# Four-token sums of q and k of the first sequence: by TensorE from the loaded rows, in place of VectorE from the transposed ones

## The chip, the cores and the metric

The kernel runs on one core of a Trainium2 chip. The metric is the time of one execution on the device in microseconds (us), the median of three runs. TensorE (PE), VectorE (DVE), ScalarE (ACT), GpSimd (POOL) and SyncE (SP) each work through a queue of their own, in order; SP only issues DMAs here.

## What is computed

Attention over 2 sequences of 576 tokens with 8 heads of width 64, then two mixtures of experts over the 1152 tokens. Cut to what matters:

```python
q_d = q.reshape(B, H, Sd, factor, D).mean(axis=3)      # factor = 4, Sd = 144
k_d = k.reshape(B, H, Sd, factor, D).mean(axis=3)
v_d = v.reshape(B, H, Sd, factor, D).mean(axis=3)
out_up = np.repeat(sm_attn(q_d, k_d, v_d), factor, axis=2)
mask = np.abs(pos[:, None] - pos[None, :]) < factor     # a narrow band
out_local = np.matmul(softmax(where(mask, scale * q @ k.T, -1e9)), v)
x = _moe_ref(out_up + out_local, **moe)                 # 4 experts, all of them for every token
return _moe2_ref(x, **moe2)                             # 8 experts, one for each token
```

## The kernel before

The attention works on pairs of heads. Pair n (0 to 3 are the first sequence, 4 to 7 the second) is loaded as `kraw` and `qraw`: each in two halves of tokens, f = 0 and 1, on 98 partitions with 3 tokens x 2 heads x 64 values each. `tr` transposes a half on TensorE in three matmuls against the identity into a bank of PSUM, `t_copy` brings the bank to SBUF as `kT` or `qT` (channels on partitions, 292 tokens), on ScalarE or VectorE.

From there two branches start. The coarse branch needs sums over four neighbouring tokens: `pool4` makes them from kT and qT, as one reduction on VectorE (L434) or two additions on GpSimd, 72 sums for each half. `down` then makes the scores of the sums (`d1_mm`, L466), their softmax (minimum on VectorE, exponentials on ScalarE, the product `da` on VectorE, L487), transposes it (`d2_tr`, L492), multiplies with the sums of v (`d3_mm`, L504) and copies to `od`. The local branch (`scores`, L544; `l2_tr`, L579; `l3_mm`, L595) makes the band's softmax in units (pair, half): (0), (1) and then (2, 3) together for half 0, (0, 1) and (2, 3) for half 1. `l3_add` joins both branches to `xf`, and `x_hi`, `x_lo` split that into `xhi`, `xlo`, the two parts in which the first mixture (L693: `mm1`, L712 to L714: `mm2`) takes its input. Slice kk of `xhi` holds pair kk; a product over all of a chunk's 512 features needs all four pairs.

The first mixture needs the weights as `w1h`, `w1l`, `w2h`, `w2l`: a copy on ScalarE (L414) and a difference on VectorE (L673), or other engines.

What sets the order is the planner `Plan`: each operation has an engine or several to choose from, a cost, what it reads and writes and a priority; `order` lists the operations as they would start by those costs, and the program issues them in that order, each engine's queue in order. While the plan's clock is under 100 us it also puts **fillers** in front of an operation of TensorE that it sees waiting: matmuls of a constant (L1590) whose result nobody reads, to keep TensorE's clock up. A buffer named in `new` is waited for by the planner; PSUM has 7 banks for it. The second sequence's attention is planned among the first mixture's products. After the plan the rest of the first mixture is a plain loop, and the second mixture has plans of its own.

Of the kernel before, what the change touches and what calls it, by code (L numbers as in the profile page):

```python
# [8 lines left out]
F32 = mybir.dt.float32  # L9
# [4 lines left out]
ALU = mybir.AluOpType  # L14
# [3 lines left out]
D = 64  # L18
HALF = S // 2
SD = S // 4  # L20
# [50 lines left out]
RP = 98  # L71
RR = 3
QOFF = S - RR * RP
# [14 lines left out]
TARGET = 3600  # L88
HARD = 3400
TRC = 1  # L90
RUNS = 0
TRR = .75
DP = (50, 20, 0)
DQ = (0, 0, 0, 0, 0, 0)
DMC = 1.23
# [195 lines left out]
def moe_chain_kernel(ctx, tc, q, k, v, probs, w1, w2, mod, wg, mbias, v1, v2, out):  # L291
    nc = tc.nc
# [12 lines left out]
    at = ctxa.enter_context(tc.tile_pool(name="at", bufs=2, side="right"))  # L305
# [7 lines left out]
    ident = const.tile([128, 128], F32, tag="ident", name="ident")  # L313
# [7 lines left out]
    def make_mask():  # L321
# [9 lines left out]
        nc.gpsimd.tensor_copy(out=mask16[0:64], in_=mask[0:64])  # L331
        nc.gpsimd.tensor_copy(out=mask16[64:128], in_=m1[64:128])

    def consts():
        P.op("Pool", .6, lambda: make_identity(nc, ident), w=["ident"], prio=-9)
        P.op("Pool", 1.2, make_mask, r=["ident"], w=["mask"], prio=-8)
        P.op("SP", .65, lambda: nc.sync.dma_start(out=p_raw, in_=probs.rearrange("(i p) e -> p i e", p=128)),
             w=["praw"], prio=8, lat=.5)
        P.op("DVE", .8, norm_p, r=["praw"], w=["p"], prio=30)
# [17 lines left out]
    T = {}  # L357
    LAST = {}

    def ch(nm, d):  # L360
        return {e: c for e, c in d.items() if (nm, e) not in NOT}


    def qk_dma(nm, src, n, f):
        b, hp = divmod(n, 4)
        if f == 0:
            T[nm, n] = at.tile([RP, 2, 2 * RR * D], F32, tag=nm + "raw", name=nm + "raw", bufs=RAWB)
        x = src[b, 2 * hp:2 * hp + 2, QOFF * f:QOFF * f + RR * RP]
        if n < RUNS:
            nc.sync.dma_start(out=T[nm, n][:, f].rearrange("p (h x) -> p h x", h=2), in_=x.rearrange("h (p r) d -> p h (r d)", r=RR))  # L370
        else:
            nc.sync.dma_start(out=T[nm, n][:, f].rearrange("p (r h d) -> p r h d", r=RR, h=2), in_=x.rearrange("h (p r) d -> p r h d", r=RR))

    def vq_dma(n):
        b, hp = divmod(n, 4)
# [12 lines left out]
    def a_load(n, pr):  # L388
        for f in range(2):
            for nm, src in (("k", k), ("q", q)):  # L390
                cost, lat = (.5, .5) if n < RUNS else (.84, .9)
                P.op("SP", cost, lambda nm=nm, src=src, f=f: qk_dma(nm, src, n, f), prio=pr, lat=lat, w=[(nm, n, f)],
                     **({"r": [(nm, n)]} if f else {"new": [(nm + "raw", (nm, n))]}))
        P.op("SP", .65, lambda: vq_dma(n), prio=pr, lat=.82, new=[("vq", ("vq", n))])

# [5 lines left out]
    def tr(nm, n, f):  # L401
        T["pt", nm, n, f] = pt = bank()
        pv = pt[:, 0:RR * RP].rearrange("c (p r) -> c r p", r=RR)
        for r in range(RR):
            x = T[nm, n][:, f]
            if n < RUNS:
                nc.tensor.transpose(pv[0:64, r, :], x[:, D * r:D * r + D], ident[:RP, :RP])
                nc.tensor.matmul(pv[64:128, r, :], x[:, D * (RR + r):D * (RR + r) + D], ident[:RP, :RP], start=True, stop=True)
            else:
                nc.tensor.transpose(pv[:, r, :], x[:, 128 * r:128 * r + 128], ident[:RP, :RP])  # L410

    def copy(e, out, in_, scale=1.0):
        if e is nc.scalar:
            e.activation(out=out, in_=in_, func=ACTF.Copy, scale=scale)  # L414
        elif scale == 1.0:
            e.tensor_copy(out=out, in_=in_)
        else:
            e.tensor_scalar(out=out, in0=in_, scalar1=scale, scalar2=None, op0=ALU.mult)

    def t_copy(e, nm, n, f):  # L420
        o = win(f, 0) - QOFF * f
        t = T[nm + "T", n, f] = at.tile([128, KW], F32, tag=f"{nm}T{f}", name=f"{nm}T{f}", bufs=(KT0, 4)[f])
        copy(e, t, T["pt", nm, n, f][:, o:o + KW], 1.0 if nm == "k" else -0.125)

    def pool4(e, nm, n, f):
        if f == 0:
# [21 lines left out]
    def a_tr(n, pr):  # L448
        for f in range(2):
            for nm in ("k", "q"):  # L450
                pt, xt = ("pt", nm, n, f), (nm + "T", n, f)
                P.op("PE", .27 if n >= RUNS else TRR, lambda nm=nm, f=f: tr(nm, n, f), cols=TRC * RR * RP * RP / 128, r=[(nm, n), (nm, n, f), "ident"],
                     new=[("ps", pt)] + ([(f"{nm}T{f}", xt)] if n > 3 else []), prio=pr)
                P.op(ch("kt", {"ACT": .3, "DVE": .38}), 0, lambda e, nm=nm, f=f: t_copy(e, nm, n, f), r=[pt], prio=pr,
                     **({"w": [xt]} if n > 3 else {"new": [(f"{nm}T{f}", xt)]}))
                P.op(ch("p4", {"DVE": .36, "Pool": .75}), 0, lambda e, nm=nm, f=f: pool4(e, nm, n, f), r=[xt], prio=pr,
                     **({"new": [(nm + "s", (nm + "s", n))]} if f == 0 else {"w": [(nm + "s", n)]}))
        P.op("Pool", VDC, lambda: a_vd(n), r=[("vq", n)], new=[("vd", ("vd", n))], prio=pr)
# [1090 lines left out]
    if True:  # L1549
        consts()  # L1550
        a_load(0, 0)
        for b in range(2):
            P.slow, P.lag, P.also = ((1.0, 0.0, {}), (SLOWB, LAGB, {"ps": ("pa",)}))[b]
            pa, pb = ((0, BP), (BQ, BR))[b]
            for us in GRP[2 * b]:
                for m in us:
                    n = 4 * b + m
# [43 lines left out]
        for s, c, f in steps[KP:]:  # L1601
# [3 lines left out]
            r = runs.index((s, c))  # L1605
# [61 lines left out]
```

## Time and profile before

| | us |
|---|---|
| median of three runs (lowest, highest) | 627.0 (625.95, 627.65) |
| the profiled execution | 624.6 |
| its span in the profile | 622.7 |
| PE busy in the span | 600.4 (96%) |
| DVE, ACT, POOL busy | 381.8, 255.2, 86.9 |
| first product of the first mixture starts | 42.37 |

The span is the profiled execution without some 2 us around it. A row of the timeline is one instruction or several of a kind in sequence: its start, how long it ran, engine, line, operation, what it writes and reads, how many records, and in brackets how long its engine sat idle just before and who ended that. Starts of neighbours on TensorE are closer than their durations, because matmuls overlap; what an instruction costs its engine is the distance to the next start. One fp32 matmul leaves two records, a transpose one.

### The profile page before, as it was taken

Reading aid. Unit: us, or ns where it says so; the run is one execution under the profiler, and the core shown is the slowest. Engines: PE = TensorE matmul, PEld = TensorE weight load, DVE = VectorE, ACT = ScalarE, POOL = GpSimd, SP = SyncE. Lnnn points to the kernel's source line nnn. Section 1 sums busy time; section 2 is a strip of 40 time slices with the busy share of each in tenths; the row PEclk is TensorE's granted clock in tenths of the full one; section 3 lists DMA queues with packets and bytes.
Section 4 is the critical chain, followed back from the end, with each engine's and each line's share of the span. In section 5 each row is a group of like instructions: output and inputs, shape, how many; then the busy total and the mean of one; then the engine's idle time right before and its main releaser. Section 6 shows DMA issues by size and latency. Waiting matters only on the chain. (4 is left out here: it accounts for less than half of the span.)

```text
span 622.7 us, 11280 instructions
## 1 busy us (share of the span) xinstructions
PE 600.4 (96%) x4265; PEld 527.5 (85%) x4270; DVE 381.8 (61%) x817; ACT 255.2 (41%) x595; POOL 86.9 (14%) x120
## 2 busy tenths in 40 slices
PE   7689999999999999999999999999999999999994
PEld 4578888889798999999989989999988898888983
DVE  4898678767525618564342455439955789669781
ACT  5855256542313411113321334313343555559581
POOL 3333113115000001000000000001130035201011
PEclk9999999999999999999999999999999999999997
DMA  7999944107511510001330345605295404867830
GB/s 148 156 219 221 234 135 136 36 2 213 168 35 61 177 34 2 1 1 52 119 101 1 102 135 173 200 5 132 42 352 193 143 15 131 286 194 254 293 136 20
DMA packets 84465, 78.67 MB, mean 126 GB/s; under 512 B 36135, under 2 KB 67248, under 8 KB 84402
## 3 DMA queue, kind: packets, MB, share of 16 engines
q1 hardware_dynamic: 82482, 73.13, 42.0%
q0 software_dynamic: 1920, 4.73, 2.2%
q8 instruction: 35, 0.57, 0.4%
q14 instruction: 28, 0.23, 0.1%
HBM read 77.49 MB, written 5.07 MB: 133 GB/s over the span
## 5 line engine op out<-in xcount | busy, mean ns | idle before, releaser
L693 PE MATMUL ps<-xhi,w1h 128*128 128x256 f32 (+1 forms) x512 | 153.8, 300 | 0.0
L693 PE MATMUL ps<-xhi,w1l 128*128 128x256 f32 (+1 forms) x512 | 151.8, 297 | 0.0
L693 PE MATMUL ps<-xlo,w1h 128*128 128x256 f32 (+1 forms) x512 | 151.6, 296 | 0.2 <-DVE xlo L609 0.2
L699 ACT ACTIVATE hh<-ps 128x256 fp32r<-128x256 f32 (+1 forms) x128 | 52.4, 410 | 209.6 <-PE ps L693 201.2
L704 DVE SCALAR_TENSOR_TENSOR hl<-ps,hh 128x256 fp32r<-128x256 f32 (+1 forms) x128 | 57.9, 454 | 121.2 <-ACT hh L699 121.0
L712 PE MATMUL ps<-w2h,hh 128*128 128x512 f32 x288 | 115.7, 402 | 0.0
L714 PE MATMUL ps<-w2h,hl 128*128 128x512 f32 x288 | 113.6, 395 | 1.2 <-DVE hl L704 1.2
L713 PE MATMUL ps<-w2l,hh 128*128 128x512 f32 x288 | 113.3, 393 | 0.0
L693 PEld LDWEIGHTS ps<-xhi,w1h 128*128 128x128 f32 x512 | 96.5, 188 | 5.9 <-issue 0.6
L693 PEld LDWEIGHTS ps<-xlo,w1h 128*128 128x128 f32 x512 | 96.4, 188 | 5.3 <-DVE xlo L609 0.4
L693 PEld LDWEIGHTS ps<-xhi,w1l 128*128 128x128 f32 x512 | 96.4, 188 | 0.0
L714 PEld LDWEIGHTS ps<-w2h,hl 128*128 128x128 f32 x288 | 54.0, 188 | 14.8 <-DVE hl L704 2.3
L712 PEld LDWEIGHTS ps<-w2h,hh 128*128 128x128 f32 x288 | 54.2, 188 | 8.0 <-issue 0.4
L713 PEld LDWEIGHTS ps<-w2l,hh 128*128 128x128 f32 x288 | 54.2, 188 | 6.9
L673 DVE TENSOR_TENSOR w2l<-raw,w2h 128x1024 fp32r<-128x1024 f32 x32 | 39.4, 1230 | 29.3 <-ACT w2h L414 29.2
L414 ACT ACTIVATE w1h<-raw 128x1024 fp32r<-128x1024 f32 x47 | 49.7, 1057 | 17.6 <-PE ps L693 14.9
L673 DVE TENSOR_TENSOR w1l<-raw,w1h 128x1024 fp32r<-128x1024 f32 x32 | 39.1, 1221 | 10.8 <-ACT w1h L414 10.1
L414 ACT ACTIVATE w2h<-raw 128x1024 fp32r<-128x1024 f32 x28 | 29.7, 1061 | 37.6 <-PE ps L714 35.6
L1222 DVE TENSOR_TENSOR w2l<-r,w2h 128x1024 fp32r<-128x1024 f32 x28 | 33.9, 1221 | 14.5 <-ACT w2h L414 14.5
L985 POOL DMA_INDIRECT tab<-tg,si x9 | 9.6, 1062 | 209.8 <-DVE tg L982 188.3
L414 ACT ACTIVATE w2h<-r 128x1024 fp32r<-128x1024 f32 x28 | 29.4, 1058 | 17.0 <-PE ps L1345 9.2
L1321 PE MATMUL ps<-xh,w1h 128*128 128x256 f32 x128 | 36.0, 281 | 0.0
(287 smaller groups left out, 933.1 us busy)
## 6 DMA issues: line engine op xcount, KB each, us to landing
raw<-in_moe_w_dram SPq DMA_DIRECT2D x85, 512.0 KB
r<-in_moe_w_dram SPq DMA_DIRECT2D x35, 512.0 KB
v<-in_v_dram SPq DMA_DIRECT2D x32, 80.0 KB
kraw<-in_k_dram SPq DMA_DIRECT2D x16, 147.0 KB
qraw<-in_q_dram SPq DMA_DIRECT2D x16, 147.0 KB
vq<-in_v_dram SPq DMA_DIRECT2D x8, 288.0 KB
ys<-y SPq DMA_DIRECT2D x9, 256.0 KB
st<-in_moe_w_gate_dram SPq DMA_DIRECT2D x4, 512.0 KB
```

The lines of the kernel that those rows point to most:

```text
L414: e.activation(out=out, in_=in_, func=ACTF.Copy, scale=scale)
L673: e.tensor_tensor(out=l, in0=W.pop(("raw", kind, s, j)), in1=h.bitcast(F32), op=ALU.subtract)
L693: nc.tensor.matmul(o, wt[:, kk, fs], xt[:, kk, :], start=(kk == 0 and m == 0), stop=(kk == KD - 1 and m == 2))
L699: nc.scalar.activation(out=hh, in_=o, func=ACTF.Relu)
L704: nc.vector.scalar_tensor_tensor(out=hl, in0=o, scalar=0.0, in1=hh.bitcast(F32), op0=ALU.max, op1=ALU.subtract)
L712: nc.tensor.matmul(a, hh[:, ts], hi[:, f % 2, :], start=(f == 0), stop=False)
L713: nc.tensor.matmul(a, hh[:, ts], lo[:, f % 2, :], start=False, stop=False)
L714: nc.tensor.matmul(a, hl[:, ts], hi[:, f % 2, :], start=False, stop=(f == NF - 1))
L985: i = nc.gpsimd.indirect_dma_start(out=tab, out_offset=bass.IndirectOffsetOnAxis(ap=Z["si"][:, t:t + 1], axis=0), in_=G["tg"][:, 3 * c + t ...
L1222: e.tensor_tensor(out=l, in0=R["raw", u], in1=h.bitcast(F32), op=ALU.subtract)
L1321: nc.tensor.matmul(pt, wt[:, kk, fs], xt[:, kk, :], start=(i == 0), stop=(i == 3 * KD - 1))
```

## The change

For the first sequence (n < 4) the sums come straight from the loaded rows. `make_pool` has GpSimd write a matrix of ones and zeros, `poolm`, that adds the right tokens; `tr` adds to the bank of half 1 six matmuls of `kraw` or `qraw` with it (three tokens of each partition for either half; together the 144 sums, at columns 300 to 443 of the bank); `pool_copy` brings the sums to `ks` or `qs` on ScalarE or VectorE; the `pool4` of these pairs goes. A memset of `qs` is GpSimd's now. The cost that the planner is told for such a `tr` rises by .75. Two options that were switched off (`RUNS`, `TRR`) go too.

```diff
-RUNS = 0
-TRR = .75
+PPN = 4
+PPC = .75
+POFF = 300
...
+    def make_pool():
+        for g in range(2):
+            off = QOFF * g - HALF * g
+            m = pool_m[:, g]
+            nc.gpsimd.memset(m, 1.0)
+            nc.gpsimd.affine_select(out=m, in_=m, pattern=[[1, RR], [-4, 72]], compare_op=ALU.is_ge, fill=0.0, base=off, channel_multiplier=RR)
+            nc.gpsimd.affine_select(out=m, in_=m, pattern=[[-1, RR], [4, 72]], compare_op=ALU.is_ge, fill=0.0, base=3 - off, channel_multiplier=-RR)
...
+        P.op("Pool", 1.6, make_pool, w=["pool"], prio=-7)
...
+        if f and n < PPN:
+            for g in range(2):
+                for r in range(RR):
+                    nc.tensor.matmul(pt[:, POFF + 72 * g:POFF + 72 * g + 72], T[nm, n][:, g, 128 * r:128 * r + 128], pool_m[:, g, r, :],
+                                     start=(r == 0), stop=(r == RR - 1))
...
+    def pool_copy(e, nm, n):
+        t = T[nm + "s", n] = at.tile([128, SD + 16], F32, tag=nm + "s", name=nm + "s")
+        if nm == "q":
+            nc.gpsimd.memset(t[:, SD:SD + 16], 0.0)
+        copy(e, t[:, 0:SD], T["pt", nm, n, 1][:, POFF:POFF + SD], 1.0 if nm == "k" else -0.125)
...
+                if n < PPN:
+                    if f:
+                        P.op({"ACT": .19, "DVE": .24}, 0, lambda e, nm=nm: pool_copy(e, nm, n), r=[pt], new=[(nm + "s", (nm + "s", n))], prio=pr)
+                    continue
                 P.op(ch("p4", {"DVE": .36, "Pool": .75}), 0, lambda e, nm=nm, f=f: pool4(e, nm, n, f), r=[xt], prio=pr,
```

Since other costs go into the planner, the order of all engines differs up to the end of the plan. Lines move by up to 19; L410 is L414 after the change, L466 L485, L544 L563, L693 L712, L1590 L1609. The program has 38 fillers instead of 30: 26 stood ahead of the first product of the first mixture and four behind its eleventh group of three, now all 38 stand ahead of it.

TensorE near the start, before the change. `kraw` and `qraw` with `ident` are transposes, `kT,qT` the local scores of pair 0, `ks,qs` the coarse scores of pair 0.

```order
31 L537 MATMUL ps<-mask_90,ident_89 128x192
32 L544 MATMUL ps<-kT_149,qT_159 64x64 x10
33 L410 MATMUL ps<-ident,qraw 128x98 x3
34 L410 MATMUL ps<-ident,kraw 128x98 x3
35 L466 MATMUL ps<-ks,qs 64x144 x6
```

The same place after it.

```order
33 L414 MATMUL ps<-ident,qraw 128x98 x3
34 L418 MATMUL ps<-poolm,qraw 128x72 x6
35 L414 MATMUL ps<-ident,kraw 128x98 x3
...
43 L556 MATMUL ps<-mask_90,ident_89 128x192
44 L563 MATMUL ps<-kT_156,qT_164 64x64 x10
45 L414 MATMUL ps<-ident,qraw 128x98 x3
46 L414 MATMUL ps<-ident,kraw 128x98 x3
47 L418 MATMUL ps<-poolm,kraw 128x72 x6
```

Half 1 of q of pair 0 with its sums, and half 0 of k of pair 1, stood behind the local scores of pair 0 and stand ahead of them now; the coarse scores come later, behind the local scores of pair 1.

TensorE where the first mixture begins, before the change. `sc` is a local softmax, `lat,v` its product with v for half 1, `xhi,w1h` the first product of the mixture.

```order
111 L595 MATMUL ps<-lat,v 64x56 x2
112 L595 MATMUL ps<-lat,v 64x57 x6
113 L595 MATMUL ps<-lat,v 64x61 x2
...
118 L410 MATMUL ps<-ident,kraw 128x98 x3
119 L693 MATMUL ps<-xhi_91,w1h 128x256
120 L693 MATMUL ps<-xlo_95,w1h 128x256
121 L693 MATMUL ps<-xhi_91,w1l 128x256
```

The same place after it; `kT_858` and `kT_922` belong to pairs 4 and 5.

```order
145 L414 MATMUL ps<-ident,qraw 128x98 x3
146 L414 MATMUL ps<-ident,kraw 128x98 x3
147 L414 MATMUL ps<-ident,qraw 128x98 x3
148 L598 MATMUL ps<-ident,sc 128x128 x3
...
151 L563 MATMUL ps<-kT_858,qT_882 64x64 x10
152 L563 MATMUL ps<-kT_922,qT_929 64x64 x10
153 L712 MATMUL ps<-xhi_92,w1h 128x256
154 L712 MATMUL ps<-xlo_96,w1h 128x256
155 L712 MATMUL ps<-xhi_92,w1l 128x256
```

All transposes and the local scores of pairs 4 and 5 now stand ahead of the first product, and no product of half 1 with v does; from there 24 matmuls of the mixture stand in a row.

## Rows read from the trace of the kernel before

**Rows 1.** Busy time by stage: start and end, length, then each engine's; PEclk, DMA.

```profile
0.00:10.00 10.00, 6.94 (x46) 3.21 (x46) 2.46 (x7) 4.23 (x15) 3.05 (x16) 1.00 0.61 131
10.00:20.00 10.00, 8.04 (x129) 6.45 (x131) 8.40 (x29) 7.84 (x40) 4.30 (x6) 1.00 1.05 171
20.00:30.00 10.00, 7.09 (x127) 5.61 (x128) 8.49 (x22) 8.47 (x46) 3.75 (x6) 0.96 0.98 146
30.00:40.00 10.00, 8.01 (x123) 5.85 (x123) 9.27 (x28) 5.05 (x23) 2.96 (x3) 0.87 1.02 260
40.00:50.30 10.30, 9.88 (x112) 8.69 (x113) 9.58 (x27) 7.90 (x31) 5.21 (x8) 1.00 0.98 185
...
60.00:140.00 80.00, 80.00 (x828) 68.81 (x827) 56.98 (x125) 38.47 (x153) 17.87 (x37) 1.00 0.42 112
...
200.00:600.00 400.00, 398.84 (x2386) 357.87 (x2384) 239.22 (x507) 154.26 (x242) 38.84 (x40) 1.00 0.41 128
```

**Rows 2.** Waits of PE up to 50.3 us: total, times, longest.

```profile
PE ps L492 <- DVE da L487: 2.4, 1, 2.4
PE ps L410 <- DMA kraw<-in_k_dram: 2.3, 2, 1.8
PE ps L595 <- DVE lat L416: 1.8, 1, 1.8
```

**Rows 3.** Timeline of PE, the first 11 us.

```profile
0.86 3.57 PE L1590 MATMUL ps<-const-bfloat16-1.0 128*128 128x512 bf16 x8 [0.86 <-PEq L1651]
4.24 0.72 PE L410 MATMUL ps<-ident,kraw 98*128 98x98 f32 x3
...
7.20 0.56 PE L544 MATMUL ps<-kT,qT 64*64 64x64 f32 x20
...
10.02 0.47 PE L410 MATMUL ps<-ident,kraw 98*128 98x98 f32 x3 [1.77 <-DMA kraw<-in_k_dram]
10.43 0.95 PE L466 MATMUL ps<-ks,qs 64*64 64x144 f32 x12
```

**Rows 4.** Timeline of PE, between 21 and 36 us.

```profile
21.22 0.82 PE L1590 MATMUL ps<-const-bfloat16-1.0 128*128 128x512 bf16 x3
21.87 0.49 PE L579 MATMUL ps<-ident,sc 128*128 128x128 f32 x3
...
26.05 0.74 PE L595 MATMUL ps<-lat,v 64*64 64x60 f32 x20
26.73 0.47 PE L410 MATMUL ps<-ident,kraw 98*128 98x98 f32 x3
...
35.37 0.95 PE L466 MATMUL ps<-ks,qs 64*64 64x144 f32 x12
```

**Rows 5.** Timeline of PE, where the first mixture begins.

```profile
42.37 0.37 PE L693 MATMUL ps<-xhi,w1h 128*128 128x256 f32 x1
...
47.51 0.42 PE L410 MATMUL ps<-ident,qraw 98*128 98x98 f32 x3
47.76 0.42 PE L410 MATMUL ps<-ident,kraw 98*128 98x98 f32 x3
...
48.43 0.47 PE L410 MATMUL ps<-ident,kraw 98*128 98x98 f32 x3
48.74 0.47 PE L410 MATMUL ps<-ident,qraw 98*128 98x98 f32 x3
...
50.25 0.39 PE L693 MATMUL ps<-xlo,w1h 128*128 128x256 f32 x1 [0.17 <-DVE xlo L609]
```

**Rows 6.** Groups by line and form up to 60 us: busy, mean ns, idle before.

```profile
L434 DVE TENSOR_REDUCE qs<-qT 128x72 f32<-128x288 f32 x11 | 4.8, 439 | 0.8 <-ACT qT L414 0.8
...
L416 DVE COPY od<-ps 128x144 f32<-128x144 f32 x2 | 0.6, 308 | 1.3 <-PE ps L504 1.3
L414 ACT ACTIVATE od<-ps 128x144 f32<-128x144 f32 x2 | 0.6, 292 | 4.8 <-PE ps L504 4.8
```

**Rows 7.** Timeline of POOL: the identity.

```profile
1.10 0.29 POOL masks.py:199 TENSOR_SCALAR_AFFINE_SELECT ident<-ident 128x128 f32<-128x128 f32 x1
```

More of the change, by code (lines that the diff above doesn't have):

```diff
@@ L332, in make_mask @@
         nc.gpsimd.tensor_copy(out=mask16[64:128], in_=m1[64:128])
+    pool_m = at.tile([RP, 2, RR, 72], F32, tag="poolm", name="poolm", bufs=1)
+    def make_pool():
[5 more added lines that the diff above has]
+            nc.gpsimd.affine_select(out=m, in_=m, pattern=[[-1, RR], [4, 72]], compare_op=ALU.is_ge, fill=0.0, base=3 - off, channel_multiplier=-RR)
     def consts():
@@ L368, in qk_dma @@
         x = src[b, 2 * hp:2 * hp + 2, QOFF * f:QOFF * f + RR * RP]
[L369 to L372, printed above, removed]
+        nc.sync.dma_start(out=T[nm, n][:, f].rearrange("p (r h d) -> p r h d", r=RR, h=2), in_=x.rearrange("h (p r) d -> p r h d", r=RR))
     def vq_dma(n):
@@ L390, in a_load @@
             for nm, src in (("k", k), ("q", q)):
-                cost, lat = (.5, .5) if n < RUNS else (.84, .9)
-                P.op("SP", cost, lambda nm=nm, src=src, f=f: qk_dma(nm, src, n, f), prio=pr, lat=lat, w=[(nm, n, f)],
+                P.op("SP", .84, lambda nm=nm, src=src, f=f: qk_dma(nm, src, n, f), prio=pr, lat=.9, w=[(nm, n, f)],
                      **({"r": [(nm, n)]} if f else {"new": [(nm + "raw", (nm, n))]}))
@@ L404, in tr @@
         for r in range(RR):
[L405 to L410, printed above, removed]
+            nc.tensor.transpose(pv[:, r, :], T[nm, n][:, f, 128 * r:128 * r + 128], ident[:RP, :RP])
+        if f and n < PPN:
[3 more added lines that the diff above has]
+                                     start=(r == 0), stop=(r == RR - 1))
     def copy(e, out, in_, scale=1.0):
@@ L451, in a_tr @@
                 pt, xt = ("pt", nm, n, f), (nm + "T", n, f)
-                P.op("PE", .27 if n >= RUNS else TRR, lambda nm=nm, f=f: tr(nm, n, f), cols=TRC * RR * RP * RP / 128, r=[(nm, n), (nm, n, f), "ident"],
+                P.op("PE", .27 + (PPC if f and n < PPN else 0), lambda nm=nm, f=f: tr(nm, n, f), cols=TRC * RR * RP * RP / 128, r=[(nm, n), (nm, n, f), "ident"] + (["pool"] if f and n < PPN else []),
                      new=[("ps", pt)] + ([(f"{nm}T{f}", xt)] if n > 3 else []), prio=pr)
```

## The prediction, on record before the result was known

> **What bounds the kernel now.** I read the table of stages first, then the waits of TensorE in the opening stage, then its timeline there. From 60 to 140 us TensorE is busy 80.00 of 80 us, and from 200 to 600 us 398.84 of 400 [rows 1]. Attention of the second sequence, weights and all copies lie beside that. So the kernel ends when TensorE has done its work, plus what TensorE lost before it had a full queue: a microsecond lost in the opening is not regained, and VectorE's or ScalarE's time counts only where it makes TensorE wait. All that the change touches lies in the opening, up to some 50 us.
>
> There TensorE is not the limit alone. Up to 50.3 us it is busy 6.94 + 8.04 + 7.09 + 8.01 + 9.88 = 39.96 us, so idle 10.3 [rows 1]. VectorE is at 8.4 to 9.6 of 10 from 10 us on. The waits have several enders: VectorE with `da` 2.4 and `lat` 1.8, the loads of k 2.3 [rows 2]. At 50.25 the slice of `xlo` for the last pair is there [rows 5], and from then on TensorE has work. Part of the busy time is fillers: the first eight take from 0.86 to 4.24, 3.4 us [rows 3], the later ones 0.22 to 0.24 each (three from 21.22 to 21.87 take 0.65 [rows 4]).
>
> This gives the account that I use. What TensorE spends on other than needed work in the opening is, before the change: 10.3 idle + 30 fillers. After it: x idle + 38 fillers + the new matmuls. Work that is only moved from one side of the first product to the other drops out.
>
> **What it removes.** Sixteen `pool4` go, fourteen of them reductions on VectorE (L434; the count is the order's) of 439 ns mean [rows 6], less by some 0.07 from start to start, so about 5.2 us; two were pairs of additions on GpSimd, off the path. **What it adds there:** eight copies of 128x144 out of PSUM. The same shape took 308 ns on VectorE and 292 on ScalarE (`od`) [rows 6]; the order puts five on VectorE (1.2 us with the same overlap) and three on ScalarE (0.9). VectorE gains 5.2 - 1.2 = 4.0 us in the opening, ScalarE loses 0.9. These are not terms of TensorE's account; they act through x.
>
> **What it adds on TensorE.** Eight times six fp32 matmuls with 72 columns and 98x128 weights: twelve records each. The trace has no such form, so bounds. Low: the fastest transposes, with the same weights and 98 columns, follow at 0.25 for three (47.51 to 47.76 [rows 5]), 0.083 a record; 72 columns in proportion 0.061, twelve of them 0.73. High: if a record costs what the slower trios show however few its columns, (48.74 - 48.43) / 3 = 0.104 [rows 5], twelve are 1.25. Nearer to the new form in columns is L595: 20 records in 26.73 - 26.05 = 0.68 [rows 4], 0.034 each with two 64-wide tiles side by side; full-width matmuls can't share, so 0.068 and twelve are 0.81. I take 0.8: **6.4 us**, bounds 5.8 to 10.0. Lower than 5.8 would need a record to cost less than its columns.
>
> TensorE: Matmul & The Clock Gate, a page of the Trainium skill, says in its section on LDWEIGHTS that loading weights takes the number of columns divided by 1.2 ns, 107 ns for 128 columns, whatever the rows. If twelve loads set the pace that would be an estimate of 1.28 us by the page, 10.3 for the eight, close to the high bound above; the trios at 0.083 and 0.104 show that loads overlap at least in part.
>
> **Fillers.** 38 instead of 30: 8 x 0.235 = **1.9 us**. They cover waits that the planner sees and cost only where TensorE would have had work; since x below counts the idle left beside them, they stand in the sum in full.
>
> **GpSimd.** The matrix is two memsets and four selects of 98x216. Those of 128x128 took 0.29 at most [rows 7], so 0.5 each by size, 3 us at most, from 1.4 to some 4.4, and the masks behind it to some 6.6. The first matmul that reads the matrix is behind the third group of transposes, and the first group starts at 4.24 [rows 3]; the masks are read by the local scores of pair 0, which now stand behind a load that landed at 10.02. Nothing. The load covers it: if the scores could start at 7.20 as before, little or nothing would be left to cover. SP's queue keeps the order of the first nine loads, and its buffers for pair 2 are given back before its turn. Nothing either.
>
> **Moved on TensorE, and x.** I follow the new order with the durations of the rows. (a) The local scores of pair 0 ran at 7.20 [rows 3]. Now half 0 of k of pair 1 is ahead in the queue and landed at 10.02 [rows 3]; with it, two fillers and the mask they run at some 11.2. VectorE's and ScalarE's first softmax starts 4 us later, and the time from 7.8 to 11 gets two copies. (b) The coarse scores of pairs 0 and 1 come together at some 16 (pair 0 at 10.43 before [rows 3]), the transposed softmax of both behind VectorE's second `da` at some 23.7. (c) The local scores of pairs 2 and 3 come at some 29; the coarse scores of pair 3 at 32 to 33 (35.37 before [rows 4]). (d) From there the chain of pair 3 is VectorE's queue, some 40 instructions for 14 us: its last `xlo` falls at some 46.5 (50.2 before [rows 5]) and the first `w1l`, queued behind it, at 48.5. The mixture starts at 48 to 49, not in pieces from 42.37 [rows 5], and then has two full groups.
>
> The idle that I find on the way: 0.9 + 0.4 at the start, 0.4 for that load, 1.5 and 0.7 ahead of transposes that wait for VectorE's `sc`, 0.9 at `da`, 0.5 at the end: x = 5, so **5.3 us saved**. It can't be under 1.3 (the start). Above 10.3 it would need VectorE, 4.0 us freer, to be later than it is; that leaves 1.3 to 8, saved 2 to 9.
>
> **Sum.** 6.4 + 1.9 - 5.3 = +3.0 us. The profiled execution has 624.6 us, its span 622.7; with +3.0 such an execution would have 627.6. The median of the runs is 627.0, 2.4 above the profiled one, so **630.0** for the median. About 0.3% (1.9 us) is what a measurement of this kernel can tell from no change.
>
> **Rivals.**
> (1) The waits shrink further: the freed 4.0 us of VectorE lie on every chain that TensorE waits for (the 2.4 at `da` and 1.8 at `lat` are VectorE's), x falls to 2, and 6.4 + 1.9 - 8.3 = 0.0: 627.0. For it: VectorE at 9.3 of 10 from 30 to 40 us [rows 1]. Against: the load at 10.02 holds the scores, and most waits in the new order are one engine waiting for one chain, not for a full queue.
> (2) Weight loads set the pace of the new matmuls: 10.0 + 1.9 - 5.3 = +6.6, 633.6. For it: the slower trios; against: the faster ones and L595. The page named above gives 10.3 and so +6.9.
> (3) Faster: the new matmuls fall into the holes. TensorE's need is not the limit of the opening, VectorE's queue is; then the last `xlo` comes earlier by VectorE's 4.0 us and the first `w1l` follows it at once. It decides if in the new kernel TensorE stands waiting for VectorE at each of the waits of [rows 2] and all 1.9 us of fillers and most of the 6.4 lie in time in which nothing else was ready: the mixture's full start then falls near 45 instead of 48.5 and the time is 3.5 lower than forecast and some more for shorter waits: -2 us, 625.0. For it: 2.4 + 1.8 us of the idle are waits for VectorE [rows 2]. Against: the account, which needs x near 0 for it, and the start alone takes 1.3.
> (4) It doesn't do what it says: the order shows the reductions gone for four pairs and kept for the second sequence, so no chance of its own.
>
> **How the numbers follow.** Forecast (+2 to +5) 0.50; (1) 0.26; (2) 0.14; (3) 0.10. Slower by over 0.3% is the forecast and (2): 0.64; within 0.3% (1): 0.26; faster (3): 0.10. For the range: x from 1.3 to 8 with 6.4 gives -0.7 to +6.0; the high price with my x gives +6.6. From -1 to +7: 626.0 to 634.0, which leaves out (3) for the most part and what lies above (2).
>
> **What would show it.** First product of the mixture at 48 to 49 and 24 of its matmuls in a row; TensorE's idle up to there near 5; the six matmuls of a sum 0.8 from first to next start; local scores of pair 0 at some 11; 60 to 140 us full as before. The forecast is wrong if idle is under 3 (then the waits were VectorE's alone), if a sum costs 1.2 (then (2)), or if TensorE has gaps behind 60 us, which I give nothing.

## The result, and the profile after

The changed kernel takes 634.98 us (median of three runs, 634.5 to 635.11) against 627.0: a ratio of 1.0128, with a 95% interval of 1.0104 to 1.0151. The forecast was 630.0 with a range up to 634.0: the sign was right, the size was not, and the time lies outside the range. The profiled execution took 634.5 us, its span is 632.8, 10.1 more than that of the kernel before. TensorE is busy 613.9 us in it (600.4 before), so its busy time grew by 13.5 us and its idle time shrank by 3.4. Ratios leave out runs that lie more than 1.5% above the fastest run of their kernel.

The table of stages of the changed kernel, with the columns of [rows 1] (stretch, length, busy time of PE, PEld, DVE, ACT, POOL, then granted clock):

```profile
0.00:10.00 10.00, 8.57 (x47) 5.13 (x48) 0.31 (x1) 2.53 (x4) 4.68 (x22) 1.00 0.62 130
10.00:20.00 10.00, 10.00 (x132) 8.74 (x131) 3.96 (x12) 6.09 (x31) 3.88 (x7) 1.00 0.81 166
20.00:30.00 10.00, 10.00 (x106) 8.60 (x104) 5.07 (x17) 5.43 (x22) 1.54 (x2) 1.00 0.77 148
30.00:40.00 10.00, 9.35 (x200) 7.31 (x196) 8.80 (x30) 7.86 (x45) 3.39 (x5) 1.00 0.95 240
40.00:50.30 10.30, 9.49 (x92) 6.75 (x92) 7.97 (x25) 8.91 (x38) 2.50 (x4) 0.83 0.79 152
50.30:60.00 9.70, 8.44 (x111) 7.41 (x109) 9.47 (x22) 4.87 (x21) 1.95 (x3) 1.00 0.65 147
60.00:70.00 10.00, 9.51 (x102) 7.91 (x101) 6.90 (x17) 5.18 (x22) 4.39 (x7) 1.00 1.04 249
70.00:80.00 10.00, 7.96 (x59) 7.26 (x58) 5.97 (x13) 3.37 (x7) 2.07 (x2) 1.00 0.96 216
80.00:140.00 60.00, 60.00 (x608) 51.42 (x607) 44.65 (x98) 28.42 (x114) 9.77 (x11) 1.00 0.31 92
```

Three things are to be seen, against [rows 1]. TensorE is full from 10 to 30 us, where it had 4.9 us idle. VectorE is busy 0.31 + 3.96 + 5.07 = 9.34 us up to 30 us, where it had 2.46 + 8.40 + 8.49 = 19.35; the reductions that are gone explain some 4 us of that. And TensorE, which was full from 60 us on, now idles 0.49 + 2.04 = 2.53 us between 60 and 80. From 50.3 to 60 us the kernel before had no idle time to speak of either; it has 1.26 us now:

```profile
50.30:60.00 9.70, 9.63 (x82) 8.17 (x83) 7.53 (x18) 5.44 (x15) 0.07 (x2) 1.00 0.95 209
```

The timeline of TensorE (start, duration, engine, line, operation, records): L418 are the new matmuls, L563 the local scores, L485 the coarse scores, L712 the first product of the mixture.

```profile
6.63 1.48 PE L418 MATMUL ps<-poolm,kraw 98*128 98x72 f32 x12
7.95 1.04 PE L1609 MATMUL ps<-const-bfloat16-1.0 128*128 128x512 bf16 x4
...
11.34 0.56 PE L563 MATMUL ps<-kT,qT 64*64 64x64 f32 x20
...
16.42 0.56 PE L563 MATMUL ps<-kT,qT 64*64 64x64 f32 x20
16.82 1.64 PE L485 MATMUL ps<-ks,qs 64*64 64x144 f32 x24
...
31.42 0.81 PE L563 MATMUL ps<-kT,qT 64*64 64x64 f32 x40
...
34.45 0.81 PE L563 MATMUL ps<-kT,qT 64*64 64x64 f32 x40
...
53.25 0.39 PE L712 MATMUL ps<-xhi,w1h 128*128 128x256 f32 x1
```

A sum costs 7.95 - 6.63 = 1.32 us from its start to the next; six of the other seven take 1.31 or 1.32, and the one at 33.03 has 1.42 to the next start. The row at 34.45 holds the local scores of the second halves of the first two pairs, third of their kind in the kernel before, at 14.29, and now fourth: 20 us later.

The new stall behind 60 us, from the waits of TensorE between 60 and 80 us (who waits for whom, total, times, longest):

```profile
PE ps L733 <- DVE hl L723: 2.0, 1, 2.0
PE ps L732 <- DVE w2l L692: 0.5, 1, 0.5
```

VectorE's timeline around the longest of them:

```profile
72.30 0.22 DVE L589 RECIPROCAL su<-su 128x10 f32<-128x10 f32 x1
75.86 0.69 DVE L425 CAST w1h<-raw 128x1024 fp32r<-128x1024 f32 x1 [3.34 <-DMA raw<-in_moe_w_dram]
76.47 0.42 DVE L723 SCALAR_TENSOR_TENSOR hl<-ps,hh 128x256 fp32r<-128x256 f32 x1
```

And TensorE's:

```profile
74.51 0.40 PE L732 MATMUL ps<-w2l,hh 128*128 128x512 f32 x1
76.94 0.50 PE L733 MATMUL ps<-w2h,hl 128*128 128x512 f32 x1 [2.04 <-DVE hl L723]
```

VectorE waits 3.34 us for a load of weights, and `hl`, which TensorE needs, is queued behind the cast that waits.

### The profile page after: what moved, and what is told of

Its sections match the earlier page's. It is cut to its first block, busy times and chain, and to the rows that moved or that the text cites. A ratio compares the mean times of both kernels' runs of the same rounds, so it can differ in the third digit from the quotient of the medians.

```text
span 632.8 us, 11467 instructions
## 1 busy us (share of the span) xinstructions
PE 613.9 (97%) x4374; PEld 539.1 (85%) x4374; DVE 378.7 (60%) x812; ACT 252.9 (40%) x590; POOL 92.4 (15%) x126
## 3 DMA queue, kind: packets, MB, share of 16 engines
HBM read 77.49 MB, written 5.07 MB: 130 GB/s over the span
## 5 line engine op out<-in xcount | busy, mean ns | idle before, releaser
L712 PE MATMUL ps<-xhi,w1h 128*128 128x256 f32 (+1 forms) x512 | 153.5, 300 | 0.0
L712 PE MATMUL ps<-xhi,w1l 128*128 128x256 f32 (+1 forms) x512 | 151.8, 296 | 0.0
L712 PE MATMUL ps<-xlo,w1h 128*128 128x256 f32 (+1 forms) x512 | 151.5, 296 | 0.0
L712 PEld LDWEIGHTS ps<-xhi,w1h 128*128 128x128 f32 x512 | 96.4, 188 | 6.2 <-issue 0.8
L712 PEld LDWEIGHTS ps<-xlo,w1h 128*128 128x128 f32 x512 | 96.4, 188 | 4.9
L712 PEld LDWEIGHTS ps<-xhi,w1l 128*128 128x128 f32 x512 | 96.4, 188 | 0.0
L692 DVE TENSOR_TENSOR w2l<-raw,w2h 128x1024 fp32r<-128x1024 f32 x32 | 40.9, 1277 | 25.4 <-ACT w2h L423 25.4
L692 DVE TENSOR_TENSOR w1l<-raw,w1h 128x1024 fp32r<-128x1024 f32 x32 | 40.4, 1263 | 10.8 <-ACT w1h L423 10.1
```

Source lines behind the costliest of these rows:

```text
L692: e.tensor_tensor(out=l, in0=W.pop(("raw", kind, s, j)), in1=h.bitcast(F32), op=ALU.subtract)
L712: nc.tensor.matmul(o, wt[:, kk, fs], xt[:, kk, :], start=(kk == 0 and m == 0), stop=(kk == KD - 1 and m == 2))
```

## The experiments

Theory P, from the account of the prediction: the new matmuls are work on TensorE's path and cost what they last. Rival O: the changed order costs the time, and the matmuls lie mostly in time that TensorE would have idled. All ratios are to the kernel before, run on the same chip at the same time; spans are those of the profiled executions, one for each kernel (622.7 before, 632.8 changed). The quoted passages say what was expected before each run.

**Columns or weights (e1).** Twice the columns for each new matmul, everything else equal.

```diff
-POFF = 300
+POFF = 296
...
-nc.tensor.matmul(pt[:, POFF + 72 * g:POFF + 72 * g + 72], T[nm, n][:, g, 128 * r:128 * r + 128], pool_m[:, g, r, :],
-                 start=(r == 0), stop=(r == RR - 1))
+nc.tensor.matmul(pt[:, POFF + 72 * g:POFF + 72 * g + 144].rearrange("c (u n) -> c u n", u=2), T[nm, n][:, g, 128 * r:128 * r + 128],
+                 pool_m[:, g, r:r + 1, :].to_broadcast([RP, 2, 72]), start=(r == 0), stop=(r == RR - 1))
```

> The changed kernel, with each new matmul over 144 columns instead of 72 (the 72 columns of the matrix twice, the second copy into columns that the next group overwrites or nobody reads); number of matmuls, weights and order are the same. In the changed kernel twelve records take 1.31 us, 0.109 each. Theory W (the load of the 98x128 weights sets the pace): the records follow each other no faster and hardly slower, until the columns themselves take longer; the coarse scores, 24 records of 144 columns in two 64-row tiles side by side, took 1.53 us there, so 0.128 for a record alone. Twelve records then take 1.4 to 1.55 us, and the kernel takes 1 to 2 us more than the changed one, 636 to 637 us. Theory C (the columns set it): twelve records take about 2.6 us, and the kernel some 10 us more, about 645 us.

From its timeline of TensorE:

```profile
16.73 1.66 PE L418 MATMUL ps<-poolm,qraw 98*128 98x144 f32 x12
18.23 0.60 PE L1609 MATMUL ps<-const-bfloat16-1.0 128*128 128x512 bf16 x2
```

Twelve records take 1.50 us, 0.125 each, against 1.31 with half the columns: theory C is out, and the price is W's. Columns are nearly free up to there. That the loads of the 98x128 weights set the pace at 72 columns is the reading that is left; no run changes the weights alone, and the transposes, with the same weights, follow at 0.083 [rows 5]. The Trainium skill, TensorE: Matmul & The Clock Gate, section LDWEIGHTS, gives columns of the weights divided by 1.2 ns, which is 107 ns for 128; the trace agrees for this form, with 1.31 / 12 = 0.109 us a record, and not for the transposes. The ratio is 1.0211 (1.0132 to 1.0289; four runs, 635.17 to 641.85), the span 633.5.

**More and fewer matmuls in the new order.** Each sum computed twice (e2):

```diff
-            for g in range(2):
+            for g in (0, 1, 0, 1):
```

> The changed kernel, with the matmuls of each sum issued twice (the second time from zero, so that the sums are the same): 24 records of 1.31 us per twelve, so 8 x 1.31 = 10.5 us more of TensorE. Theory P (the new matmuls lie on the path, microsecond for microsecond): the median rises by 9 to 11 us over the changed kernel's 635.0, to 644 to 646 us, and the first product of the mixture starts some 9 to 11 us later than 53.25. Rival H (they lie mostly in time in which TensorE had nothing else, and what the change costs comes from the new order): it rises by less than 5 us, under 640 us, and idle time of TensorE up to the first product falls from 4.1 us to nearly nothing.

The time rises to 644.41 us (four runs, 642.02 to 652.0), ratio 1.0259 (1.0176 to 1.0342), span 643.8. Its profiled execution ran at half speed in the first 14 us (the first 24 records took 5.08 us, the second 24 3.2 at mixed speed), so its start of the mixture, 67.0, can't be compared with 53.25. By the ratios (1.0259 against 1.0128) 8 us of the 10.5 arrive, with some 5 either way: P rather than H.

And none at all, with 144 transposed columns copied in the place of the sums (e3):

```diff
-        if f and n < PPN:
-            for g in range(2):
-                for r in range(RR):
-                    nc.tensor.matmul(pt[:, POFF + 72 * g:POFF + 72 * g + 72], T[nm, n][:, g, 128 * r:128 * r + 128], pool_m[:, g, r, :],
-                                     start=(r == 0), stop=(r == RR - 1))
...
-        copy(e, t[:, 0:SD], T["pt", nm, n, 1][:, POFF:POFF + SD], 1.0 if nm == "k" else -0.125)
+        copy(e, t[:, 0:SD], T["pt", nm, n, 1][:, 0:SD], 1.0 if nm == "k" else -0.125)
```

> The changed kernel without the new matmuls; the copies of the sums read columns of the transposed tokens instead, so the coarse attention computes with numbers that are no sums. Order and all else are the same. Theory P: TensorE loses 10.5 us of work; the first product of the mixture starts 7 to 10.5 us earlier than 53.25, at 43 to 46, and the time is 7 to 10 us under the changed kernel's 635.0, at 625 to 628, near the kernel before. Rival H: less than 5 us are won, and 630 us or more remain. Since the routing behind 200 us hangs on the values, the start of the mixture decides where the two disagree.

The span is 630.3, ratio 1.0146 (1.0083 to 1.0208): 2.5 us won of 10.5 by the spans, rival H. The profiled execution is the fastest of its five runs (632.02 to 635.97); by the ratios, 1.0146 against 1.0128, nothing is won at all. From its table of stages:

```profile
20.00:30.00 10.00, 8.59 (x150) 6.35 (x152) 4.23 (x16) 5.01 (x20) 2.76 (x4) 1.00 0.73 141
30.00:40.00 10.00, 5.99 (x109) 4.43 (x102) 9.19 (x30) 8.36 (x45) 1.98 (x2) 0.80 0.97 245
```

And from its timeline of TensorE, the start of the mixture:

```profile
51.51 0.38 PE L707 MATMUL ps<-xhi,w1h 128*128 128x256 f32 x1
```

Where the matmuls were, TensorE now waits: 4.0 us idle from 30 to 40 us, at a granted clock of 0.80, and the mixture starts 1.7 us earlier only. VectorE is still little used up to 30 us (4.23 of 10 from 20 on) and nearly full behind it (9.19 of 10). So without any of the new work on TensorE, and without the reductions on VectorE, this order needs 7.6 us more than the kernel before. (Its numbers are no sums, so the routing behind 200 us is another; e9 below has the same flaw and the time of the kernel before.) Adding work to it costs nearly in full, taking work away wins little: my reading is that two limits lie close together in it.

**The same work in the old order.** These are edits of the kernel before, whose planner keeps its costs. First the matrix, built behind the masks, and the matmuls, unused (e5):

```diff
         for r in range(RR):
...
                 nc.tensor.transpose(pv[:, r, :], x[:, 128 * r:128 * r + 128], ident[:RP, :RP])
+        if f and n < 4:
+            for g in range(2):
+                for r in range(RR):
+                    nc.tensor.matmul(pt[:, 300 + 72 * g:300 + 72 * g + 72], T[nm, n][:, g, 128 * r:128 * r + 128], pool_m[:, g, r, :],
+                                     start=(r == 0), stop=(r == RR - 1))
```

> The kernel before, in its own order and with its reductions on VectorE, and in addition the new matrix and the 48 new matmuls of the first sequence, whose results nobody reads. Theory P (the new matmuls lie on TensorE's path in any order): 8 x 1.31 = 10.5 us of work, of which the 10.3 us of idle time up to 50 us may take some: 6 to 10.5 us more than the kernel before. Rival O (the new order is what costs, as the run without the matmuls let me think, which won only some 2.5 us): most of the 10.5 us disappear in the idle time, 0 to 4 us more than before.

Span 625.9, 3.2 over the kernel before, as rival O has it. But that is the fastest of four runs, 627.56 to 643.09, and the ratio is 1.0119 (1.0026 to 1.0213); this run decides nothing by itself. Now the sums are used as well, and the reductions are gone (e6):

```diff
         copy(e, t, T["pt", nm, n, f][:, o:o + KW], 1.0 if nm == "k" else -0.125)
+        if f and n < 4:
+            t = T[nm + "s", n] = at.tile([128, SD + 16], F32, tag=nm + "s4", name=nm + "s")
+            if nm == "q":
+                nc.gpsimd.memset(t[:, SD:SD + 16], 0.0)
+            copy(nc.vector, t[:, 0:SD], T["pt", nm, n, 1][:, 300:300 + SD], 1.0 if nm == "k" else -0.125)
...
     def pool4(e, nm, n, f):
+        if n < 4:
+            return
```

> The change itself, but in the order of the kernel before: the sums of the first sequence come from TensorE, right behind the transposes, and are copied by VectorE behind the copy of the transposed tokens, where the second reduction stood; the reductions are gone; the planner works with the costs of the kernel before, so nothing else moves and the fillers stay at 30. Theory O (order and fillers are the larger part of the 8 us): 0 to 4 us more than the kernel before. Theory P (the matmuls are it): 6 to 10 us more, as in the changed kernel. Between the run with unused matmuls and this one lies what the reductions' absence is worth: up to 4 us.

Span 624.4, ratio 1.0051 (1.0004 to 1.0098), within what theory O expected. Here too the profiled execution is the fastest; the ten runs reach from 626.24 to 643.8 with a median of 631.77 (the kernel before beside them 624.87 to 633.7, median 627.06), so by the medians it is 4.7 us, a little above O's 4. Its stages:

```profile
10.00:20.00 10.00, 9.22 (x143) 8.34 (x143) 5.08 (x17) 6.36 (x34) 3.53 (x6) 1.00 0.88 157
20.00:30.00 10.00, 9.94 (x146) 8.46 (x147) 7.39 (x21) 8.04 (x39) 3.28 (x6) 1.00 0.70 149
30.00:40.00 10.00, 9.95 (x178) 8.55 (x170) 8.62 (x30) 6.68 (x32) 1.98 (x2) 1.00 0.95 243
```

In this execution most of the 10.5 us of matmuls went into TensorE's idle time (7.09 and 8.01 busy in [rows 1], now 9.94 and 9.95), and the granted clock, 0.96 and 0.87 there, is 1.00: an estimate from these shares is that the matmuls won back up to 0.4 + 1.3 us of slow clock as well. The same without matmuls and matrix (e9):

```diff
-            copy(nc.vector, t[:, 0:SD], T["pt", nm, n, 1][:, 300:300 + SD], 1.0 if nm == "k" else -0.125)
+            copy(nc.vector, t[:, 0:SD], T["pt", nm, n, 1][:, 0:SD], 1.0 if nm == "k" else -0.125)
```

> The order of the kernel before with neither reductions nor new matmuls: VectorE copies 144 transposed columns where the sums would be, so the coarse attention computes with numbers that are no sums. It completes the square of two orders, each with and without the matmuls (old order with them: span 624.4 in the profiled execution; new order with them 632.8, without them 630.3). Theory O (the order costs 6 to 8 us by itself, the matmuls 2 to 3 in either order): 621 to 623 us of span, so 1.5 to 3.5 under the old order with the matmuls. Rival P (what the matmuls cost was hidden in the old order by the reductions' absence): 617 to 619 us of span.

Span 622.7, exactly that of the kernel before, ratio 1.0008 (0.9990 to 1.0025). Theory O. It says two things more. The reductions that are gone, the whole gain that the change could have on VectorE, are worth nothing in this order. Of its stages:

```profile
10.00:20.00 10.00, 8.12 (x105) 6.41 (x105) 5.41 (x14) 5.37 (x31) 4.96 (x8) 0.66 0.88 170
20.00:30.00 10.00, 9.21 (x148) 7.23 (x149) 8.46 (x25) 8.95 (x44) 2.04 (x3) 1.00 0.81 153
30.00:40.00 10.00, 7.32 (x126) 5.46 (x124) 9.47 (x34) 6.87 (x35) 2.05 (x3) 1.00 0.98 261
```

VectorE's relief falls into 10 to 20 us (5.41 against 8.40 in [rows 1]), ahead of the stretch in which it is full. And TensorE ran at a clock of 0.66 from 10 to 20 us without a visible effect on the end: it isn't the limit there in this order. Last, the sums of the last two pairs alone, with `n in (2, 3)` in the three places (e11):

```diff
-        if f and n < 4:
+        if f and n in (2, 3):
```

> The order of the kernel before, with the sums of only the last two pairs of the first sequence from TensorE, and the reductions of the first two pairs left on VectorE. TensorE's idle time in the kernel before is 2.9 us from 20 to 30 us and 2.0 from 30 to 40, with the granted clock at 0.96 and 0.87; these matmuls, 4 x 1.31 = 5.2 us, fall there, and VectorE is at 8.5 to 9.3 of 10 there. Theory O: the same time as before or up to 2 us less, 0.997 to 1.000 of it. Rival P: half of the matmuls' 10.5 us on the path, 3 to 5 us more, 1.005 to 1.008.

Ratio 1.0021 (1.0005 to 1.0037), span 623.5: between the two, and no gain either.

By spans, the square is: old order without the new matmuls 622.7 and with the sums 624.4; new order without them 630.3 and with the sums 632.8. The matmuls cost 1.7 and 2.5 us, the order, with its eight additional fillers, 7.6 and 8.4. Each span is one execution, and in all four corners the fastest of its kernel. By the ratios the square is 1.0008 and 1.0051, 1.0146 and 1.0128: the order costs 0.8 to 1.4%, 5 to 9 us (3 at the least, if e6 is taken by the median of all its runs), and the matmuls 0.4% in the old order and nothing that can be told in the new. Either way the order is the larger part; how much larger is open.

**What in the order.** First what the planner was told: a higher cost of a sum (e4), then the columns of the new matmuls for its choice of fillers (e8).

```diff
-PPC = .75
+PPC = 1.32
```

> The changed kernel, with the planner told 1.32 us for a sum instead of 0.75, near the 1.31 that the trace shows; the order changes. Theory P (the cost is TensorE's own work): hardly anything is won, 633 to 636 us. Rival O (a good part of the 8 us comes from an order that was planned with a wrong cost, the gaps of 2.5 us between 60 and 80 us among it): 630 to 632 us, and TensorE is full from 60 to 80 us.

Ratio 1.0167 (1.0096 to 1.0239), span 631.5: hardly anything is won, and TensorE still idles 1.0 us from 60 to 70. The wrong cost alone isn't what hurts.

```diff
-cols=TRC * RR * RP * RP / 128
+cols=TRC * RR * RP * RP / 128 + (2400 if f and n < PPN else 0)
```

> The changed kernel, with the planner told that the new matmuls occupy TensorE (2400 columns per step for the count from which it decides on fillers; in the changed kernel it counts only the transposes): 15 fillers instead of 38, and another order, near that of the kernel before. Theory F (the fillers are on the path): 23 x 0.235 = 5.4 us less than the changed kernel, 629 to 630 us. Theory P: 8 x 1.31 us stay in it, with idle time where the fillers were, 633 us or more.

Ratio 1.0120 (1.0012 to 1.0228), span 632.5. This decides nothing: the four runs reach from 631.79 to 642.4, and in the profiled execution TensorE lost 4.6 us between 200 and 600 us, where it loses some 1.2 in most others; without that loss the span would be some 629, near what F expected. The next run (e12) tests the fillers by themselves: the 28 behind 7 us are left out of the changed kernel.

```diff
-                    dummies(P.fill[i])
+                    dummies(P.fill[i] if t < 7 else 0)
```

> The changed kernel with the ten fillers up to 7 us alone; the other 28, 28 x 0.235 = 6.6 us, are left out, the order of the rest is the same. Theory F (each filler stands in TensorE's time in full, as the prediction had it): 5 to 6.6 us less than the changed kernel, span 626 to 628. Rival G (they lie in waits, or the granted clock falls without them): at most 2 us less, span 631 or more, with a granted clock below 1 in more of the opening.

Slower: ratio 1.0216 (1.0184 to 1.0248), span 637.3, rival G and beyond it. From its stages:

```profile
8.00:10.00 2.00, 1.57 (x15) 1.42 (x13) 0.31 (x1) 0.81 (x2) 0.51 (x1) 1.00 1.11 177
10.00:12.00 2.00, 1.72 (x30) 1.31 (x31) 0.93 (x3) 0.65 (x3) 1.56 (x4) 0.99 1.15 184
12.00:14.00 2.00, 2.00 (x12) 2.00 (x11) 0.00 (x0) 1.09 (x7) 0.00 (x0) 0.50 1.10 188
14.00:16.00 2.00, 2.00 (x12) 2.00 (x12) 0.46 (x1) 0.48 (x4) 0.00 (x0) 0.50 0.97 179
```

From its timeline of TensorE, a sum in this stretch:

```profile
12.27 2.72 PE L418 MATMUL ps<-poolm,kraw 98*128 98x72 f32 x12
14.78 0.70 PE L414 MATMUL ps<-ident,qraw 98*128 98x98 f32 x3
```

After two stretches with 1.57 and 1.72 us busy in 2, the granted clock falls to 0.50, 1.2 GHz, and a sum takes 14.78 - 12.27 = 2.51 us instead of 1.31. It falls to 0.50 again near 44 and 54 us. The fillers, taken together, pay for themselves here; what the eight additional ones do was not run by itself.

Then three priorities in the changed kernel, each alone. The local scores of the first pair ahead of transposes of equal due time (e7):

```diff
-                scores([(4 * b + m, 0) for m in us], pa + us[0] + OG)
+                scores([(4 * b + m, 0) for m in us], pa + us[0] + OG - (.1 if b == 0 and us == (1,) else 0))
```

> The changed kernel with one priority altered: the local scores of the first pair go ahead of transposes of the same due time. In the changed kernel the planner had a tie there, since a step of transposes and sums together is 1.02 us long and cannot be divided, and took the longer step first; the scores ran at 11.34 instead of 7.20. Fillers are 34 instead of 38. Theory S (the late start of VectorE and ScalarE, 4 us, is what the run without matmuls still paid): the scores run near 9, the opening is 2 to 4 us shorter, 631 to 633 us. Rival P (TensorE's own work): at most the four fillers are won, 634 us or more.

The scores ran at 9.39, as expected; ratio 1.0075 (1.0028 to 1.0123), span 629.7: 3.1 us of span won, theory S. The first segment's weights earlier (e13):

```diff
-WPR = 9
+WPR = 6
```

> The changed kernel with the priority of the first segment's weights raised (6 instead of 9), so that the first low part of weights is made some 7 us earlier in the planner's order and the fourth load of weights can be issued some 7 us earlier; 33 fillers. Theory L (the late low part holds the three load buffers, the next weights come when the loads of the second sequence fill the DMA engines, and TensorE waits for them between 60 and 80 us): TensorE is full from 60 to 80 us, idle there under 0.5 us instead of 2.5, and the span falls by 2 to 4 us, to 629 to 631. Rival: the stalls stay or come back elsewhere in the opening, span 632 or more.

Ratio 1.0072 (1.0045 to 1.0098). The span, 631.0, is that of its longest run: the first 13 us of the profiled execution were at half speed (a sum of twelve records from 7.76 to 10.28). TensorE is full between 60 and 80 us:

```profile
60.00:70.00 10.00, 10.00 (x88) 8.76 (x87) 7.83 (x18) 3.75 (x10) 4.29 (x6) 1.00 1.05 230
70.00:80.00 10.00, 10.00 (x81) 8.98 (x80) 7.96 (x20) 3.83 (x12) 1.29 (x1) 1.00 1.08 247
```

Theory L holds for the gap. And the local scores of the second halves of the first two pairs, which the change had moved from 14.29 to 34.45 (e14):

```diff
-                scores([(4 * b + m, 1) for m in us], pb + us[0] + OG)
+                scores([(4 * b + m, 1) for m in us], pb + us[0] + OG - (4 if b == 0 and us == (0, 1) else 0))
```

> The changed kernel with one priority altered: the local scores of the second halves of the first two pairs are due 4 steps earlier, so that the planner puts them behind the first halves' scores (near 17 to 18 us instead of 34.45), as in the kernel before (14.29); 37 fillers. Theory V (without this work VectorE and ScalarE stand idle up to 30 us, and it then lies on their full queue behind 30 us): VectorE is busy 13 us or more up to 30 us instead of 9.3, the span falls by 3 to 6 us from 632.8, to 627 to 630. Rival (the loss is elsewhere): span 631 or more.

Span 624.2, 8.6 under the changed kernel and more than theory V had expected; ratio 1.0044 (1.0016 to 1.0072) against 1.0128, so 5 us by the times (ten runs, 625.94 to 633.6, median 627.79 beside 626.32 of the kernel before). Its stages:

```profile
0.00:10.00 10.00, 8.21 (x46) 4.85 (x46) 0.31 (x1) 2.52 (x4) 4.61 (x22) 1.00 0.60 128
10.00:20.00 10.00, 10.00 (x163) 8.50 (x162) 3.81 (x11) 5.68 (x30) 4.01 (x7) 1.00 0.86 176
20.00:30.00 10.00, 10.00 (x111) 8.25 (x109) 8.76 (x29) 8.37 (x42) 2.00 (x2) 1.00 0.68 140
30.00:40.00 10.00, 10.00 (x164) 8.12 (x160) 8.32 (x27) 7.68 (x34) 3.38 (x5) 1.00 0.93 251
40.00:50.30 10.30, 10.30 (x186) 7.89 (x187) 10.07 (x33) 9.05 (x39) 3.18 (x6) 1.00 0.82 157
...
60.00:70.00 10.00, 10.00 (x86) 9.21 (x85) 7.21 (x16) 4.68 (x17) 2.01 (x4) 1.00 1.08 244
70.00:80.00 10.00, 10.00 (x67) 9.06 (x66) 6.41 (x10) 3.46 (x7) 1.99 (x2) 1.00 0.79 243
```

And the moved scores in its timeline of TensorE:

```profile
19.01 0.81 PE L564 MATMUL ps<-kT,qT 64*64 64x64 f32 x40
```

VectorE has 8.76 us of work from 20 to 30 us where it had 5.07, up to 30 us 12.88 (a little under the 13 expected), TensorE is full from 10 to 50.3 us, its clock 1.00 throughout, and the gap between 60 and 80 us is gone although the fourth load of weights comes at 56.60, only 2.3 us earlier. All 48 new matmuls are in this kernel, and 37 of the 38 fillers: by themselves these can't be the loss. Two combinations remain, the first of the two priorities of scores (e15):

```diff
-                scores([(4 * b + m, 0) for m in us], pa + us[0] + OG)
+                scores([(4 * b + m, 0) for m in us], pa + us[0] + OG - (.1 if b == 0 and us == (1,) else 0))
...
-                scores([(4 * b + m, 1) for m in us], pb + us[0] + OG)
+                scores([(4 * b + m, 1) for m in us], pb + us[0] + OG - (4 if b == 0 and us == (0, 1) else 0))
```

> The run with the second halves' scores early, and in addition the first pair's local scores ahead of transposes of the same due time (which alone gave a span of 629.7); 27 fillers. Theory V with both: the order is then near that of the kernel before, and the span near the 624.4 that the old order gives with the same sums: 624 to 627. Rival: 629 or more, as with the first pair's scores alone.

The second with the weights besides, and 3 steps for 4 (e16):

```diff
-WPR = 9
+WPR = 6
```

> As the run with both scores early, with the first segment's weights raised as well (priority 6 instead of 9; alone it gave a span of 631.0 and no gap between 60 and 80 us) and the second halves' scores 3 steps earlier instead of 4. Theory V: 623 to 626; if the three causes add up it reaches the old order's 624.4. Rival: the weights' halves now stand in VectorE's full queue ahead of attention, 627 or more.

They give 1.0038 (1.0014 to 1.0061) with a span of 623.5, and 1.0034 (1.0014 to 1.0055) with a span of 629.5 in an execution whose clock was 0.67 from 40 to 50.3 us. Neither is told apart from e14 by the times; the three priorities don't add up. None of these kernels beats the kernel before.

## Why the prediction was wrong

**The price of a sum** was the first term that failed. 8 x 0.8 = 6.4 was taken from L595's row, and the high bound, 1.25 a sum, from the slower trios; measured were 1.31, so 10.5 us, above the high bound of 10.0 too. Rival 2 was right that columns don't set the price (e1); that the weight loads do is its reading, not shown by itself. Columns in proportion were the wrong scale for 72 columns on 128 columns of weights.

**The moves on TensorE** were the step that decides. The account lets work that is only moved drop out, so the new order had no price of its own; the runs give it 7.6 us of span without any of the new matmuls (e3 against e9). Of the moves listed as (a) to (d), the first three came within 3 us of the forecast: local scores of the first pair at 11.34, coarse scores at 16.82, the softmax's transposes at 25.93, local scores of pairs 2 and 3 at 31.42; of (d), the 24 matmuls in a row came, but at 53.25 instead of 48 to 49. The list leaves out the local scores of the second halves of the first two pairs, at 14.29 before and at 34.45 now. They were VectorE's and ScalarE's work up to 30 us; without it VectorE was busy 9.3 of 30 us there and then 26.2 of 30. The kernel before had 19.4 and then 26.4: behind 30 us there was little room to make up for what was missed. e14 puts them back and the order's loss is gone from the span. That it goes by way of VectorE's work is read from the stages; e14 also changes what the planner puts behind these scores. The start of the mixture is not where the loss shows: in e14 it is hardly earlier, at 52.46, but TensorE has had other work up to there and has it behind.

**x**, the idle of TensorE in the opening, was forecast as 5 (its seven parts add up to 5.3, so 5.0 saved and not 5.3) and is 1.43 + 0.65 + 0.81 = 2.9 up to 50.3 us, 4.1 up to the mixture's start: inside the bounds, near enough. But it was read as time saved. e3 shows that it was only covered: take the matmuls away and TensorE waits in their place. The 10.3 us of idle before were a little too many as well. Of the 30 fillers the trace has all 30 weight loads but only 25 matmuls, so five records are missing:

```profile
L1590 PE MATMUL ps<-const-bfloat16-1.0 128*128 128x512 bf16 x25 | 8.8, 485 | 1.0 <-PEq L1651 0.9
L1590 PEld LDWEIGHTS <-const-bfloat16-1.0 128*128 128x128 bf16 x30 | 3.3, 118 | 4.1 <-issue 3.2
```

Right behind three of the loads that have no matmul, the timeline of TensorE shows idle gaps of 0.16, 0.22 and 0.25 us, some 0.6 in all.

**The fillers**, 1.9 us in full, were counted rightly and most likely priced wrongly: in this kernel leaving 28 of them out costs 4.5 us of span (e12). **VectorE's 4.0 us** were not a term, but behind rivals 1 and 3; in the old order they are worth nothing (e9). **Behind 60 us** the prediction gave nothing; 2.5 us are lost there in the changed order, in two other orders of it none (e13, e14).

**The account itself** adds up: 10.5 + 1.9 - 7.4 of idle + 1.2 from 50.3 to 60 + 2.5 from 60 to 80 = 8.7 of the 10.1 us of span. Of the other 1.4, some 0.6 are the missing records just named and 0.4 is idle time between 140 and 200 us; the rest I can't attribute. Yet the same kind of account, drawn up for the old order, would name the same 10.5 us of matmuls, and there they cost 1.7. An account of where TensorE's time lies is not a statement of what gives it back.

The direction was right partly by luck: the matmuls do have a price, and no gain on VectorE stands against it, but the larger part of the time comes from the order, which the forecast's account left out. What remains open: the three priorities each win 3 us or more alone (e7 and e14 by the spans, e13 by the ratio) and not more together than the best of them, so what they win overlaps, and the loss can't be shared out among the steps of the order. The runs show what TensorE lacked: it is busy 38.7 of the 44 us from 36 to 80 in the changed kernel and 43.8 in e14.

## What to carry to other kernels

Where a change alters the order, list for each engine which groups of work crossed a boundary of stages, by comparing starts of every group and not only of those near the edit: the loss was in a group that the diff doesn't mention. Before pricing new work on the engine that bounds the kernel, run the same work in the old order and the new order without the work; two runs told more here than all terms of the sum. Take several runs of each: the profiled execution was the fastest of its kernel in all four corners of the square, and its medians are less clear. For a short matmul with full-width weights, take the price by records and not by columns, and leave fillers out only if the granted clock holds without them.

## What the runs showed of the hardware

- One record of an fp32 matmul with 98x128 weights follows the last at 0.109 us with 72 columns and 0.125 with 144, and at 0.209 with 72 where the granted clock was 0.50 (e12): at half the clock the price nearly doubles.
- Work that looks useless can buy its own time: the granted clock from 20 to 40 us rose from 0.96 and 0.87 to 1.00 when the matmuls filled the holes (e6), and it was 0.50 from 12 to 16 us when the fillers were taken out (e12).
- Some profiled executions run at half speed up to 10 to 14 us (e1, e2, e13), while the clock column shows 1.00 there: the distance of known instructions shows it (a sum took 2.52 us in e13, from 7.76 to 10.28, and 1.32 later). Two spans are compared better when these distances have been compared first.
- Sums in the unused columns of a bank tie the copies of that bank together. The rows are from the changed kernel; the transposes of this bank start at 6.32 and the sums at 6.63:

```profile
6.32 0.47 PE L414 MATMUL ps<-ident,kraw 98*128 98x98 f32 x3
8.15 0.41 ACT L423 ACTIVATE kT<-ps 128x292 f32<-128x292 f32 x1 [1.96 <-PE ps L418]
8.59 0.31 DVE L425 COPY ks<-ps 128x144 f32<-128x144 f32 x1 [8.59 <-ACT kT L423]
```

ScalarE's copy of the transposed tokens starts only when the sums are done, some 1.3 us after the transposes, and VectorE's copy of the sums only when ScalarE's copy is done, 0.4 us later. (The 8.59 in brackets is VectorE's whole time from the start of the span: this copy is its first instruction.) The Trainium skill, PSUM — Partial Sum Buffer, section PSUM bank collisions raise a hardware error, has the rule that two engines must not be at one bank and quadrant at once; in these rows they aren't. What these waits cost was not tried; the old order with the sums (e6) has them too.
